# Fused chunk attention, gated mixing and feed-forward: a gate through tanh, the norm's Newton steps on GpSimd, totals of squares with bf16 ones

## The chip, the cores and the metric

One core of a Trainium2 chip. The time is the device time of one execution in microseconds; the kernel before has a median of 771.5 us over three runs (769.86 to 771.7).

## The reference, cut to what matters

```python
# attention: 4 batches, 8 heads, 768 tokens, head size 64; chunks of 32 queries, each
# sees 16 tokens to the left, its own 32, 8 to the right and 8 memory keys
a = np.exp(scores - max); out = (a / (a.sum() + 1e-9)) @ v_full
x = out as [4, 768, 512]
# gated mixing
gate_pre = sum over k of conv_w[k] * xp[:, k:k+S, :]        # 5 taps
gate = 1.0 / (1.0 + np.exp(-gate_pre))
x = gate * (x @ w_val) @ w_out
# norm and feed-forward
xn = (x - mu) / np.sqrt(var + 1e-06) * g_ln
return x + np.maximum(xn @ w_ch1, 0.0) @ w_ch2              # 512 -> 2048 -> 512
```

## The kernel before

The 3072 tokens are cut into 24 sub-blocks of 128 tokens, and these into 13 blocks: the first and the last have one sub-block, the eleven between have two. Nearly every matmul takes operands that were split into a high and a low float16 half (three products for one), with power-of-two scales that come from sums of squares.

Three streams work on each block. `attention` (from line 222) handles one sub-block in eight steps: sums of squares on ScalarE, their total over the partitions by a matmul with a tile of ones (`totals`, line 127, tile `tot`), the split of q, k and v, the scores, an Exp on ScalarE (line 286), the softmax, and the product with v. Its probabilities `p` go through a DMA transpose to `pT` before the product `pv`. `mix` (line 356) computes the five taps of the gate into `gt` (lines 366 and 370), a Sigmoid over it (line 373), the value product `val` (line 386), their product (line 388), its split into `hg` (lines 391 and 392), the output product `yps` (line 403), and then the norm of each sub-block: `y` (line 408), `bn_stats` and `bn_aggr` to `mv` (lines 411 and 412), the variance `va` (414), a first guess `rt` of 1/sqrt from the exponent bits (417 and 419), three Newton steps on it (422 to 424), all on [128, 1] tiles on VectorE, and the normalised row `xh` (427), which is split into two halves (438 on ScalarE, 439 on VectorE) and goes through two DMA transposes to `xn`. The halves have one buffer, so that those of a block's second sub-block wait for the transposes of the first. `ffn` works on chunks of hidden features: `ch1` fills one of two PSUM banks `c_ps` (line 458), ScalarE and VectorE evict it as the two halves of `h` (lines 461 and 463), and `ch2` multiplies them with the second weight into `acc` (line 478). The last chunk of a block has no later product to hide behind: its `ch2` follows the one before it at once. Of each three products of `ch2` the first two take the half of `h` that ScalarE writes, the third the one of VectorE.

The streams are laid out as generators; two strings, `PLAN` for the opening and `STEADY` for each later block, say in which order their steps are issued, mixing one block ahead of the feed-forward and attention two. A scheduler then sets the final order on each engine, and each engine runs its list in order. During the opening the weights, which arrive as float64 words, are turned into float32 (lines 148 and 149), summed (`gram`) and split (lines 198 and 199).

GpSimd has little to do: constants at the start, a maximum over the partitions (line 522), and one small copy or memset per sub-block (lines 314 and 316).

```python
for _ in range(3):
    nc.vector.scalar_tensor_tensor(out=tt, in0=rt, scalar=rt, in1=va, op0=ALU.mult, op1=ALU.mult)
    nc.vector.tensor_scalar(out=tt, in0=tt, scalar1=-0.5, scalar2=1.5, op0=ALU.mult, op1=ALU.add)
    nc.vector.tensor_tensor(out=rt, in0=rt, in1=tt, op=ALU.mult)
```

Of the kernel before, what the change touches and what calls it, by code (L numbers as in the profile page):

```python
# [18 lines left out]
P = 128  # L19
LEFT, RIGHT, CHUNK, MEM = 16, 8, 32, 8  # L20
PSCALE = 14
MID = 15
# [19 lines left out]
def passes(a, b):  # L42
    """The products that make up a @ b: of two whole operands the one, of two operands
    that were split into a high and a low half all but that of the low halves."""
    return [(a[0], b[0])] if len(a) == 1 else [(a[i], b[j]) for i, j in PASSES]
# [3 lines left out]
def chunk_attention_moe_kernel(ctx: ExitStack, tc: tile.TileContext,  # L49
# [31 lines left out]
    # ---------------------------------------------------------------- constants  # L81
    ones = const.tile([P, P], F32, name="ones")
# [10 lines left out]
    # Weights: n pieces of 1024 columns. Float32 piece i lies in slots 2i+1 and 2i+2; its  # L93
    # halves (float16) take slots 2i and 2i+1, the second one written over its source.
# [21 lines left out]
    # Powers of two from sums of squares: s with |x| s <= 2**bits for every x of the  # L116
    # sum, and 1/s, both put together from the exponent bits.
# [8 lines left out]

    def totals(cols, n):
        t = ps.tile([P, 512], F32, tag="ps", name="tot")
        nc.tensor.matmul(out=t[:, 0:n], lhsT=ones, rhs=cols, start=True, stop=True)
        return t[:, 0:n]  # L130

    # float64 to float32. The words are loaded from two bytes on, so that of each number
    # the first word holds bits 47..16 and the next 16 bits are the top: sign, 11 bits of
    # exponent, 4 of mantissa. Read as bfloat16 and written as float16, the top loses the
    # three bits of exponent that float32 lacks; the rest of the mantissa then joins it.
# [17 lines left out]
    # Room for a raw piece: most of them wait in the slots of the last weight.  # L153
# [14 lines left out]
    # Sum of squares of all pieces: the diagonal of their products with themselves.  # L168
    def gram(W, j):
# [4 lines left out]
        # the upper halves of the words, bfloat16 cut off below, are near enough for a scale  # L174
# [5 lines left out]
    def weight_scale(W, bits, name, factor=None):  # L180
# [8 lines left out]
        nc.tensor.matmul(out=W.acc[:, P:P + 1], lhsT=ones, rhs=col, start=True, stop=True)  # L189
# [11 lines left out]
    # ---------------------------------------------------------------- attention  # L201
    # A block is one or two sub-blocks of 128 tokens, whatever their batches.
# [19 lines left out]
    def attention(n, d, u):  # L222
        """Steps of one sub-block of 128 tokens (two groups of two chunks, four pairs of
        heads); x lands in place u of block d."""
# [49 lines left out]
        # A chunk sees 64 of its group's 96 keys: the first chunk the first 64, the second the last.  # L274
# [12 lines left out]
        # keys before the sequence and behind it were filled with its own: they count for nothing  # L287
# [56 lines left out]
    # ---------------------------------------------------------------- gated mixing, norm  # L344
# [11 lines left out]
    def mix(j):  # L356
# [16 lines left out]
        nc.scalar.activation(out=gt[:, :, 0:T], in_=gt[:, :, 0:T], func=AF.Sigmoid)  # L373
# [6 lines left out]
        for w in range(2):  # L380
            t = ps.tile([P, 2, 256], F32, tag="ps", name="val")
            for u in range(2):
                fc = 2 * w + u
                todo = [p for kc in range(KC) for p in passes(Wv.rows(kc, split, fc * P, P), [x[:, kc, 0:T] for x in d["x"]])]
                for x, (l, r) in enumerate(todo):
                    nc.tensor.matmul(out=t[:, u, 0:T], lhsT=l, rhs=r, start=(x == 0), stop=(x == len(todo) - 1))  # L386
            fs = slice(2 * w, 2 * w + 2)
            nc.vector.scalar_tensor_tensor(out=gt[:, fs, 0:T], in0=t[:, :, 0:T], scalar=2.0 ** -MID if split else 1.0,  # L388
                                           in1=gt[:, fs, 0:T], op0=ALU.mult, op1=ALU.mult)
            if split:  # L390
                nc.scalar.activation(out=h[0][:, fs, 0:T], in_=gt[:, fs, 0:T], func=AF.Copy)  # L391
                nc.vector.tensor_tensor(out=h[1][:, fs, 0:T], in0=gt[:, fs, 0:T], in1=h[0][:, fs, 0:T],
                                        op=ALU.subtract)
# [288 lines left out]
```

## Time and profile before

| | |
|---|---|
| timed runs | 771.5 us median (769.86 to 771.7) |
| span of the profiled execution, first to last instruction | 772.0 us; it has no separate device time |
| PE busy | 719.4 us (93%), 6412 matmuls |
| PEld (weight loads) busy | 503.0 us (65%) |
| DVE (VectorE) busy | 552.7 us (72%), 1308 instructions |
| ACT (ScalarE) busy | 456.0 us (59%), 758 instructions |
| POOL (GpSimd) busy | 9.0 us (1%), 35 instructions |
| chain that ended last | PE 73%, DVE 12%, ACT 9%, issue 4%, DMA 2% |
| granted TensorE clock, mean | 0.969 |

PE is TensorE's matmuls, L458 is line 458 of the kernel before. Busy time alone does not tell what bounds a stretch: the timeline of the stretch and the waits in it do. Ends of matmuls are modelled in the profile; the distance from one start to the next is what a matmul in a row costs.

### The profile page before, as it was taken

The page shows a single profiled execution, that of the slowest core. Times are in us where ns is not written, and L with a number is a line of the kernel's source. Part 1 is how long each engine was busy: PE and PEld are TensorE (multiplying, and loading weights), DVE is VectorE, ACT ScalarE, POOL GpSimd, SP SyncE. Part 2 cuts the span into 40 slices and gives each one's busy share as a digit, 9 for nine tenths or more (in the row PEclk, how much of TensorE's full clock was granted, in tenths as well). Part 3 has the DMA queues.
Part 4 walks back from the last instruction along what each step waited for, and adds up shares of the span by engine and source line. Part 5 has one row for each costly group of instructions (what it writes and reads, how often), then busy time and mean ns, then how long its engine had stood idle before and what let it go on. Part 6 is the DMA issues. An engine that isn't in the chain of part 4 may idle for free.

```text
span 772.0 us, 15717 instructions
## 1 busy us (share of the span) xinstructions
PE 719.4 (93%) x6412; PEld 503.0 (65%) x6412; DVE 552.7 (72%) x1308; ACT 456.0 (59%) x758; POOL 9.0 (1%) x35
## 2 busy tenths in 40 slices
PE   1567996999999999999999999999999999999997
PEld 1446853665776776766767766766766766766675
DVE  3788998898776876876876886786786787672321
ACT  5997995876773763764764664674575564531110
POOL 2000000000000000000000000000000000000000
PEclk9685997999999999999999999999999999999999
DMA  7877624214213223223223122223223111011010
GB/s 291 310 306 286 246 62 91 76 44 101 90 50 89 69 74 71 63 76 70 62 76 70 62 77 69 69 79 74 62 79 84 45 27 44 15 21 35 2 42 14
DMA packets 69735, 68.92 MB, mean 89 GB/s; under 512 B 53280, under 2 KB 53280, under 8 KB 69664
## 3 DMA queue, kind: packets, MB, share of 16 engines
q1 hardware_dynamic: 69376, 67.91, 29.6%
q8 instruction: 50, 0.82, 0.4%
q14 instruction: 21, 0.17, 0.1%
q10 hardware_dynamic: 288, 0.02, 0.0%
HBM read 49.30 MB, written 6.29 MB: 72 GB/s over the span
## 4 chain that ended last, share of the span: by engine, by line
PE 73%; DVE 12%; ACT 9%; issue 4%; DMA 2%; POOL 0%; DVEq 0%; POOLq 0%; ACTq 0%
PE c_ps L458 29%; PE acc L478 27%; PE yps L403 7%; PE val L386 4%; PE s_ps L268 3%; DVE gt L370 2%; PE pv L325 2%; DMA xn<-xh 1%; ACT top L148 1%; DVE w L149 1%; ACT w L198 1%; DMA pT<-p 1%; DVE w L199 1%; ACT sc L280 1%; ACT L286 1%
## 5 line engine op out<-in xcount | busy, mean ns | idle before, releaser
L478 PE MATMUL acc<-w,h 128*128 128x512 f16 (+1 forms) x1136 | 266.0, 385 | 0.2 <-DVE h L463 0.2
L458 PE MATMUL c_ps<-xn,w 128*128 128x256 f16 (+1 forms) x2304 | 258.8, 270 | 6.5 <-DMA xn<-xh 6.5
L458 PEld LDWEIGHTS <-w 128*128 128x128 f16 x2304 | 217.2, 99 | 44.5 <-DMA xn<-xh 7.3
L478 PEld LDWEIGHTS <-h 128*128 128x128 f16 x1104 | 106.4, 98 | 113.6 <-DVE h L463 0.7
L461 ACT ACTIVATE h<-c_ps 128x512 f16<-128x512 f32 (+1 forms) x96 | 56.7, 590 | 81.1 <-PE c_ps L458 80.0
L463 DVE SCALAR_TENSOR_TENSOR h<-c_ps,h 128x512 f16<-128x512 f32 x92 | 63.1, 685 | 52.8 <-ACT h L461 52.7
L370 DVE SCALAR_TENSOR_TENSOR gt<-xT,cw_sb,gt 128x256 f32<-128x256 f32 (+1 forms) x208 | 82.3, 455 | 0.1
L403 PE MATMUL yps<-wo,hg 128*128 128x512 f16 x276 | 63.5, 379 | 0.0
L386 PE MATMUL val<-x,wv 128*128 128x256 f16 (+1 forms) x576 | 62.4, 268 | 0.5 <-ACT x L340 0.5
L386 PEld LDWEIGHTS <-wv 128*128 128x128 f16 x576 | 54.4, 98 | 7.0 <-issue 0.7
L280 ACT ACTIVATE sc<-s_ps 64x256 f32<-64x256 f32 x96 | 36.3, 378 | 24.8 <-PE s_ps L268 23.9
L234 ACT ACTIVATE vs<-vt 128x1024 bf16<-128x1024 f32 x24 | 25.1, 1048 | 42.3 <-PE pv L325 40.7
L403 PEld LDWEIGHTS <-hg 128*128 128x128 f16 x276 | 26.9, 100 | 29.6
L268 PE MATMUL s_ps<-ks,bd 128*128 128x96 f16 x576 | 32.1, 215 | 11.6 <-ACT bd L249 8.0
L485 DVE SCALAR_TENSOR_TENSOR y<-acc,co_w,y 128x512 f32<-128x512 f32 x23 | 16.3, 747 | 36.9 <-PE acc L478 36.9
L268 PEld LDWEIGHTS <-bd 128*128 128x128 f16 x576 | 30.1, 103 | 16.3 <-issue 12.9
L438 ACT ACTIVATE xh<-xh 128x512 f16<-128x512 f32 x23 | 14.3, 623 | 43.3 <-DVE xh L427 40.1
L249 ACT ACTIVATE bd<-qt,s 64x512 f16<-64x512 f32 x48 | 34.2, 713 | 5.0 <-DVE s L122 4.3
L250 DVE SCALAR_TENSOR_TENSOR bd<-qt,s,bd 64x512 f16<-64x512 f32 x48 | 35.7, 743 | 1.1 <-ACT bd L249 0.3
L391 ACT ACTIVATE hg<-gt 128x512 f16<-128x512 f32 (+1 forms) x24 | 14.6, 611 | 31.7 <-DVE gt L388 31.6
L335 DVE TENSOR_SCALAR xT<-pv,c_pv 64x256 f32<-64x256 f32 x44 | 19.7, 489 | 19.0 <-ACT xT L333 18.7
L258 DVE SCALAR_TENSOR_TENSOR vs<-vt,s,vs 128x1024 f16<-128x1024 f32 x24 | 30.7, 1278 | 0.3 <-ACT vs L257 0.3
(119 smaller groups left out, 813.5 us busy)
## 6 DMA issues: line engine op xcount, KB each, us to landing
vt<-in_v_dram SPq DMA_DIRECT2D x24, 512.0 KB, 4.1
kt<-in_k_dram SPq DMA_DIRECT2D x24, 384.0 KB, 3.7
w<-in_w_ch_dram SPq DMA_DIRECT2D x8, 1023.8 KB, 8.0
qt<-in_q_dram SPq DMA_DIRECT2D x24, 256.0 KB, 2.7
out_dram<-y SPq DMA_DIRECT2D x24, 256.0 KB, 2.0
w<-in_w_ch_dram SPq DMA_DIRECT2D x5, 1023.5 KB, 7.1
raw<-in_w_ch_dram SPq DMA_DIRECT2D x3, 1023.5 KB, 11.2
w<-in_w_val_dram SPq DMA_DIRECT2D x2, 1023.5 KB, 9.0
```

The lines of the kernel that those rows point to most:

```text
L249: nc.scalar.activation(out=hi, in_=src, func=AF.Copy, scale=s[pp, 0:1])
L250: nc.vector.scalar_tensor_tensor(out=lo, in0=src, scalar=s[pp, 0:1], in1=hi, op0=ALU.mult, op1=ALU.subtract)
L258: nc.vector.scalar_tensor_tensor(out=v2[1], in0=vt, scalar=s[:, 2:3], in1=v2[0], op0=ALU.mult, op1=ALU.subtract)
L268: nc.tensor.matmul(out=t[:, hp, :], lhsT=bd[r0][:, hp, g].rearrange("p c e q -> p (c e q)"), rhs=k2[r1][:, hp, g, :], start=(x == 0), stop ...
L280: nc.scalar.activation(out=by_group[pp, :, g, :], in_=s_ps[g][pp, :, ch * CHUNK:ch * CHUNK + NSEEN], func=AF.Copy)
L370: nc.vector.scalar_tensor_tensor(out=o, in0=xT[:, hp, 0:n, kk:kk + SUB], scalar=cw_sb[:, kk, hp:hp + 1], in1=o, op0=ALU.mult, op1=ALU.add)
L386: nc.tensor.matmul(out=t[:, u, 0:T], lhsT=l, rhs=r, start=(x == 0), stop=(x == len(todo) - 1))
L403: nc.tensor.matmul(out=t, lhsT=l, rhs=r, start=(x == 0), stop=(x == len(todo) - 1))
L458: nc.tensor.matmul(out=t[:, u * T:(u + 1) * T], lhsT=l, rhs=r, start=(x == 0), stop=(x == len(todo) - 1))
L461: nc.scalar.activation(out=h[0], in_=t, func=AF.Relu)
L463: nc.vector.scalar_tensor_tensor(out=h[1], in0=t, scalar=0.0, in1=h[0], op0=ALU.max, op1=ALU.subtract)
L478: nc.tensor.matmul(out=a, lhsT=l, rhs=r, start=(m == 0 and x == 0), stop=(m == NM - 1 and x == len(todo) - 1))
```

## The change

Three edits; no comment or empty line that was taken out counts.

1. The gate. The Sigmoid becomes Tanh with a scale of 0.5, the product with `val` becomes (1 + tanh) times `val`, and the half goes into a later factor (`cy_w`, or 0.5 for the first block); the factor 2^-MID moves into the two splitting instructions, with MID at 16 for 15.
2. The norm. The three Newton steps move from VectorE (three instructions a step) to GpSimd (four a step, twelve per sub-block); the first guess takes one VectorE instruction for two.
3. The totals. The tile of ones is bfloat16, and the matmul reads the upper halves of the float32 words of the sums as bfloat16; the same for the totals of the weights.

```diff
-    ones = const.tile([P, P], F32, name="ones")
+    ones = const.tile([P, P], BF16, name="ones")
+    def upper(cols):
+        return cols.bitcast(BF16).rearrange("p (n w) -> p n w", w=2)[:, :, 1]
...
-        nc.tensor.matmul(out=t[:, 0:n], lhsT=ones, rhs=cols, start=True, stop=True)
+        nc.tensor.matmul(out=t[:, 0:n], lhsT=ones, rhs=upper(cols), start=True, stop=True)
...
-        nc.scalar.activation(out=gt[:, :, 0:T], in_=gt[:, :, 0:T], func=AF.Sigmoid)
+        nc.scalar.activation(out=gt[:, :, 0:T], in_=gt[:, :, 0:T], func=AF.Tanh, scale=0.5)
...
-            nc.vector.scalar_tensor_tensor(out=gt[:, fs, 0:T], in0=t[:, :, 0:T], scalar=2.0 ** -MID if split else 1.0,
-                                           in1=gt[:, fs, 0:T], op0=ALU.mult, op1=ALU.mult)
+            nc.vector.scalar_tensor_tensor(out=gt[:, fs, 0:T], in0=gt[:, fs, 0:T], scalar=1.0, in1=t[:, :, 0:T],
+                                           op0=ALU.add, op1=ALU.mult)
             if split:
-                nc.scalar.activation(out=h[0][:, fs, 0:T], in_=gt[:, fs, 0:T], func=AF.Copy)
-                nc.vector.tensor_tensor(out=h[1][:, fs, 0:T], in0=gt[:, fs, 0:T], in1=h[0][:, fs, 0:T],
-                                        op=ALU.subtract)
+                nc.scalar.activation(out=h[0][:, fs, 0:T], in_=gt[:, fs, 0:T], func=AF.Copy, scale=2.0 ** -MID)
+                nc.vector.scalar_tensor_tensor(out=h[1][:, fs, 0:T], in0=gt[:, fs, 0:T], scalar=2.0 ** -MID,
+                                               in1=h[0][:, fs, 0:T], op0=ALU.mult, op1=ALU.subtract)
...
-            nc.vector.tensor_scalar(out=tt.bitcast(I32), in0=va.bitcast(I32), scalar1=1, scalar2=None,
-                                    op0=ALU.logical_shift_right)
-            nc.vector.tensor_scalar(out=rt.bitcast(I32), in0=tt.bitcast(I32), scalar1=-1.0,
+            nc.vector.tensor_scalar(out=rt.bitcast(I32), in0=va.bitcast(I32), scalar1=-0.5,
                                     scalar2=float(0x5f3759df), op0=ALU.mult, op1=ALU.add)
             for _ in range(3):
-                nc.vector.scalar_tensor_tensor(out=tt, in0=rt, scalar=rt, in1=va, op0=ALU.mult, op1=ALU.mult)
-                nc.vector.tensor_scalar(out=tt, in0=tt, scalar1=-0.5, scalar2=1.5, op0=ALU.mult, op1=ALU.add)
-                nc.vector.tensor_tensor(out=rt, in0=rt, in1=tt, op=ALU.mult)
+                nc.gpsimd.tensor_tensor(out=tt, in0=rt, in1=rt, op=ALU.mult)
+                nc.gpsimd.tensor_tensor(out=tt, in0=tt, in1=va, op=ALU.mult)
+                nc.gpsimd.tensor_scalar(out=tt, in0=tt, scalar1=-0.5, scalar2=1.5, op0=ALU.mult, op1=ALU.add)
+                nc.gpsimd.tensor_tensor(out=rt, in0=rt, in1=tt, op=ALU.mult)
```

The order of the instructions, first on VectorE, at the second norm of a block in the later part (`mv` and `va` are the mean and variance, `rt` and `tt` the Newton step's tiles, `h` the evicted chunk, the last three rows the normalised row and its low half and the block's last chunk). Before, from the first guess of `rt` on:

```order
L419 TENSOR_SCALAR rt<-tt 128x1
L422 SCALAR_TENSOR_TENSOR tt<-rt,va 128x1
L423 TENSOR_SCALAR tt<-tt 128x1
L424 TENSOR_TENSOR rt<-rt,tt 128x1
L422 SCALAR_TENSOR_TENSOR tt<-rt,va 128x1
L423 TENSOR_SCALAR tt<-tt 128x1
L463 SCALAR_TENSOR_TENSOR h<-c_ps,h 128x512
L424 TENSOR_TENSOR rt<-rt,tt 128x1
L422 SCALAR_TENSOR_TENSOR tt<-rt,va 128x1
L423 TENSOR_SCALAR tt<-tt 128x1
L424 TENSOR_TENSOR rt<-rt,tt 128x1
L427 TENSOR_SCALAR xh<-y,mv,rt 128x512
```

Now, in the changed kernel, whose lines stand five further down from here on (L423 is the first guess, L432 the row `xh`, L444 its low half, L468 the eviction of `h`):

```order
L417 BN_AGGR mv<-bs 128x2
L422 TENSOR_SCALAR va<-mv 128x1
L423 TENSOR_SCALAR rt<-va 128x1
L468 SCALAR_TENSOR_TENSOR h<-c_ps,h 128x512
L432 TENSOR_SCALAR xh<-y,mv,rt 128x512
L444 TENSOR_TENSOR xh_3690<-xh,xh_3689 128x512
L468 SCALAR_TENSOR_TENSOR h<-c_ps,h 128x512
```

Between the guess and `xh` only one eviction is left on VectorE, and the block's last eviction stands behind `xh` and its low half.

At the first norm of the same block, now:

```order
L423 TENSOR_SCALAR rt<-va 128x1
L468 SCALAR_TENSOR_TENSOR h<-c_ps,h 128x512
L432 TENSOR_SCALAR xh<-y,mv,rt 128x512
L288 TENSOR_REDUCE mx<-sc 128x8
L444 TENSOR_TENSOR xh_3624<-xh,xh_3623 128x512
L289 TENSOR_TENSOR sc<-sc,mx 128x512
```

The two softmax instructions (L288 and L289, lines 284 and 285 before) stood ahead of `xh` in the kernel before and stand behind it now.

On GpSimd, at the first norm of the program:

```order
L318 MEMSET xT 128x4x4
L320 COPY xT<-xT 128x4x4
L426 ISA
L426 TENSOR_TENSOR tt<-rt 128x1
L427 TENSOR_TENSOR tt<-tt,va 128x1
L428 TENSOR_SCALAR tt<-tt 128x1
L429 TENSOR_TENSOR rt<-rt,tt 128x1
```

The row ISA, which loads code, is new and stands once; the four rows behind it are one of the three Newton steps, and each of the twelve instructions waits for the one before it.

On ScalarE the 26 table loads of the kernel before (`ACT_TABLE_LOAD`, one at the start, then one ahead of each Sigmoid and one ahead of the next Exp) become one, at the start. On PE the order is the same from the third block's feed-forward on; ahead of that some products have changed places.

## Rows read from the trace of the kernel before

**Rows 1.** Busy time per stretch; columns: us, PE, PEld, DVE, ACT, POOL busy, PEclk, DMA share, GB/s

```profile
0.00:193.00 193.00, 145.69 (x1327) 106.08 (x1327) 159.23 (x351) 150.82 (x228) 5.87 (x18) 0.88 0.53 181
193.00:680.00 487.00, 485.74 (x4375) 337.53 (x4376) 364.98 (x882) 290.37 (x508) 3.17 (x17) 1.00 0.25 65
```

**Rows 2.** What PE waited for from 193 us on: total, times, longest

```profile
PE pv L325 <- DMA pT<-p: 0.8, 1, 0.8
```

**Rows 3.** Timeline of PE in one later block: start us, us, instruction, count

```profile
280.49 0.28 PE L129 MATMUL tot<-ss,ones 128*128 128x3 f32 x2
280.63 2.75 PE L403 MATMUL yps<-wo,hg 128*128 128x512 f16 x12
...
299.86 5.34 PE L478 MATMUL acc<-w,h 128*128 128x512 f16 x24
305.14 0.87 PE L325 MATMUL pv<-pT,vs 64*128 64x64 f16 x48
```

**Rows 4.** Timeline of DVE in the same block: start us, us, instruction, [idle before]

```profile
270.78 0.69 DVE L296 TENSOR_REDUCE sum<-sc 128x8 f32<-128x512 f32 x1 [1.34 <-ACT sc L286]
...
271.95 0.69 DVE L299 TENSOR_TENSOR sc<-sc,rs 128x512 f32<-128x512 f32 x1
273.33 0.69 DVE L302 TENSOR_TENSOR p<-sc,p 128x512 f16<-128x512 f32 x1 [0.69 <-ACT p L301]
...
287.21 0.15 DVE L417 TENSOR_SCALAR tt<-va 128x1 int32<-128x1 int32 x1
...
290.37 0.69 DVE L285 TENSOR_TENSOR sc<-sc,mx 128x512 f32<-128x512 f32 x1
...
291.91 0.69 DVE L296 TENSOR_REDUCE sum<-sc 128x8 f32<-128x512 f32 x1 [0.39 <-ACT sc L286]
...
294.93 0.69 DVE L302 TENSOR_TENSOR p<-sc,p 128x512 f16<-128x512 f32 x1
295.55 0.17 DVE L412 BATCH_NORM_AGGREGATE mv<-bs 128x2 f32<-128x6 f32 x1
...
295.94 0.15 DVE L417 TENSOR_SCALAR tt<-va 128x1 int32<-128x1 int32 x1
...
298.70 0.55 DVE L427 TENSOR_SCALAR xh<-y,mv,rt 128x512 f32<-128x512 f32 x1
299.99 0.69 DVE L439 TENSOR_TENSOR xh<-xh,xh 128x512 f16<-128x512 f32 x1 [0.74 <-ACT xh L438]
300.69 0.69 DVE L463 SCALAR_TENSOR_TENSOR h<-c_ps,h 128x512 f16<-128x512 f32 x1
```

**Rows 5.** Timelines of ACT, DVE and PE around the second block's norm, same columns

```profile
110.59 1.28 ACT L286 ACT_TABLE_LOAD   x1
...
112.18 0.15 DVE L414 TENSOR_SCALAR va<-mv 128x1 f32<-128x1 f32 x1
...
118.00 0.54 DVE L427 TENSOR_SCALAR xh<-y,mv,rt 128x512 f32<-128x512 f32 x1
...
120.72 0.55 DVE L427 TENSOR_SCALAR xh<-y,mv,rt 128x512 f32<-128x512 f32 x1
...
128.90 4.84 PE L458 MATMUL c_ps<-xn,w 128*128 128x256 f16 x23 [1.92 <-DMA xn<-xh]
```

**Rows 6.** Groups by line: the table loads ahead of the Sigmoids; busy us, mean ns

```profile
L373 ACT ACT_TABLE_LOAD x13 | 16.7, 1283 | 0.2
```

**Rows 7.** Timelines of POOL and DVE: start us, us, instruction, [idle before]

```profile
22.61 0.45 POOL L522 PARTITION_ALL_REDUCE g_max<-g_one  x1 [6.30 <-DVE wv_col L186]
...
38.91 0.20 POOL L316 COPY xT<-xT 128x16 f32<-128x16 f32 x1 [15.80 <-ACT xT L333]
...
99.04 0.11 POOL L314 MEMSET xT<- 128x16 f32 x1 [8.27 <-DVE gt L370]
...
307.57 0.90 DVE L335 TENSOR_SCALAR xT<-pv,c_pv 64x256 f32<-64x256 f32 x2 [1.56 <-ACT xT L333]
308.52 0.20 POOL L316 COPY xT<-xT 128x16 f32<-128x16 f32 x1 [27.57 <-DVE xT L335]
```

More of the change, by code (lines that the diff above doesn't have):

```diff
@@ L21 @@
 PSCALE = 14
-MID = 15
+MID = 16
 NTOP = 2
@@ L188, in weight_scale @@
             nc.vector.tensor_tensor(out=col, in0=col, in1=factor, op=ALU.mult)
-        nc.tensor.matmul(out=W.acc[:, P:P + 1], lhsT=ones, rhs=col, start=True, stop=True)
+        nc.tensor.matmul(out=W.acc[:, P:P + 1], lhsT=ones, rhs=upper(col), start=True, stop=True)
         pow2(W.acc[:, P:P + 1], 1, bits, s, inv)
@@ L403, in mix @@
                 nc.tensor.matmul(out=t, lhsT=l, rhs=r, start=(x == 0), stop=(x == len(todo) - 1))
-            c_y = 1.0
+            c_y = 0.5
             if split:
@@ L413, in mix @@
             va = sm_p.tile([P, 1], F32, tag="va", name="va")
-            nc.vector.tensor_scalar(out=va, in0=mv[:, 1:2], scalar1=1e-6, scalar2=None, op0=ALU.add)
             rt = sm_p.tile([P, 1], F32, tag="rt", name="rt")
             tt = sm_p.tile([P, 1], F32, tag="tt", name="tt")
-            nc.vector.tensor_scalar(out=tt.bitcast(I32), in0=va.bitcast(I32), scalar1=1, scalar2=None,
-                                    op0=ALU.logical_shift_right)
-            nc.vector.tensor_scalar(out=rt.bitcast(I32), in0=tt.bitcast(I32), scalar1=-1.0,
+            nc.vector.tensor_scalar(out=va, in0=mv[:, 1:2], scalar1=1e-6, scalar2=None, op0=ALU.add)
+            nc.vector.tensor_scalar(out=rt.bitcast(I32), in0=va.bitcast(I32), scalar1=-0.5,
                                     scalar2=float(0x5f3759df), op0=ALU.mult, op1=ALU.add)
             for _ in range(3):
-                nc.vector.scalar_tensor_tensor(out=tt, in0=rt, scalar=rt, in1=va, op0=ALU.mult, op1=ALU.mult)
-                nc.vector.tensor_scalar(out=tt, in0=tt, scalar1=-0.5, scalar2=1.5, op0=ALU.mult, op1=ALU.add)
-                nc.vector.tensor_tensor(out=rt, in0=rt, in1=tt, op=ALU.mult)
+                nc.gpsimd.tensor_tensor(out=tt, in0=rt, in1=rt, op=ALU.mult)
+                nc.gpsimd.tensor_tensor(out=tt, in0=tt, in1=va, op=ALU.mult)
+                nc.gpsimd.tensor_scalar(out=tt, in0=tt, scalar1=-0.5, scalar2=1.5, op0=ALU.mult, op1=ALU.add)
+                nc.gpsimd.tensor_tensor(out=rt, in0=rt, in1=tt, op=ALU.mult)
             yield
@@ L551, in mixing_weights @@
             so, io = weight_scale(Wo, 15, "wo")
-            nc.vector.tensor_scalar(out=cy_w, in0=iv, scalar1=io, scalar2=2.0 ** MID, op0=ALU.mult, op1=ALU.mult)
+            nc.vector.tensor_scalar(out=cy_w, in0=iv, scalar1=io, scalar2=2.0 ** (MID - 1), op0=ALU.mult, op1=ALU.mult)
             yield
```

## The prediction

> **What bounds the kernel now.** I read the busy times of two stretches first. From 193 us to 680 us PE is busy for 485.74 of 487.00 us at a granted clock of 1.00, while DVE has 364.98 and ACT 290.37 [rows 1]. Nothing is gained there by relieving DVE or ACT: only what shortens PE's own row of products counts, or a new wait of PE. Before 193 us PE has 145.69 of 193 us at a mean clock of 0.88, DVE 159.23 and ACT 150.82: here PE waits, and work taken off the other two can come through. The second view is what PE waited for from 193 us on: one wait above half a microsecond, 0.8 us on the transposed probabilities [rows 2]. Then I read one later block on PE and DVE [rows 3, 4], because the change puts a chain of twelve GpSimd instructions into DVE's order, and the block's last eviction stands behind it. Last come the norm of the second block in the opening [rows 5], the table loads [rows 6], and the few things that GpSimd does today [rows 7]. The sum is made against the span of 772.0 us, which is 0.5 us above the median of the timed runs; a difference under 0.3%, 2.3 us, cannot be told from none.
>
> **Totals.** A total starts at 280.49 and the next product at 280.63 [rows 3]: 0.14 us for two passes over 128x3 columns. One pass is left, which now loads its weights: between half of it and all of it is saved, 0.07 to 0.14; I take 0.10, nearer to half. Seventeen of the 24 totals lie behind 193 us: 17 x 0.10 = **-1.7 us** (1.2 to 2.4).
>
> **Table loads.** Thirteen stand ahead of the Sigmoids, 1.283 us each [rows 6], and 13 others ahead of an Exp or at the start; one load remains in all. Behind 193 us ACT has some 197 us free, and the loads that go there were hidden by PE. Only the 0.8 us wait on `pT` [rows 2] has two of them upstream, in the Sigmoid and the Exp of the same block: 2 x 1.283 is more than 0.8, so I take **-0.8 us** (0 to 0.8).
>
> The Trainium skill, "ScalarE: Activation LUTs", section "What ACT_TABLE_LOAD costs", puts a switch of tables at about 1283 ns and a drain of about 1380 ns besides. The rows have the 1283; no row here has a drain as an entry of its own. By the page the switch that leaves the opening's path would give 1.4 us more, and the sum would be 766.1.
>
> **The opening.** The second block's feed-forward takes its last `xn` at 128.90, after PE has been idle 1.92 us [rows 5]. Ahead of it stand, in one chain, an Exp's table load (1.28 at 110.59), `va` at 112.18, and the two `xh` at 118.00 and 120.72. Between `va` and the first `xh` lie 5.8 us of DVE work, among them 20 small instructions of both norms' Newton steps, which I put at 0.08 us each net of their overlap, 1.6 us (bound: 0.15 each, 3.0, as the first guess takes [rows 4]). With the load and these gone the first `xh` starts some 3 us earlier, near 115.0. The halves of the second `xh` wait for the transposes of the first, so that the second follows by the same amount. The first block's norm, at 55 to 67 us, holds 1.5 us more of the same kind upstream. Together **-4.5 us**. The ends: -1.0, if other DVE work fills the gaps, and -6.5, if the small instructions cost their full duration and all idle time goes. It is less by whatever the GpSimd chain takes above the 2.95 us that I put in below.
>
> **The chain on GpSimd.** DVE loses ten short instructions a sub-block; from 193 us on that is work off the path, worth nothing. In their place `xh` waits for twelve GpSimd instructions, each behind its predecessor, and DVE goes in order: behind `xh` are queued its low half and the eviction of the block's last `h`, for which PE waits. I call C the time from the end of the first guess to the start of `xh`. In the block shown [rows 4] the first guess would end at 287.36 (start 287.21 plus 0.15). From there to the block's last eviction the new order has, by the spacings of today's rows: first C; `xh` to its low half 1.29 (298.70 to 299.99); on to the softmax's subtraction 0.62 (294.93 to 295.55, as between two full instructions); subtraction to sum, with the Exp between, 1.54 (290.37 to 291.91); sum to the scaled row 1.17 (270.78 to 271.95); to `p` 1.38 (271.95 to 273.33); to `mv` 0.62; `mv` to the end of the second guess 0.54 (295.55 to 296.09). These are 7.16. Then C again, and from `xh` to the end of `h` 1.29 + 0.70 + 0.69 = 2.68. So the last `h` is ready at 287.36 + 7.16 + 2.68 + 2C = 297.2 + 2C. PE needs it at the third product of the second half of its last 24, the 15th: 299.86 + 14 x 0.22 (5.28 / 24) = 302.9 [rows 3], and 0.1 sooner for the total. **Up to C = 2.80 us nothing is lost; above it the block loses twice the rest.** There are ten such blocks: nine of two sub-blocks behind 193 us, and the one just before.
>
> What is C? Today GpSimd has no arithmetic on such tiles. The nearest rows are a copy of 128x16, 0.20 us, which starts 0.05 after the DVE instruction it waits for ends (308.47 to 308.52), and a memset of 128x16, 0.11 us [rows 7]. Reading one operand thus costs at most 0.09. A step with one operand is then about 0.23 with its hand-over (C = 2.81 if all twelve were so cheap), one with two operands up to 0.32. Nine of the twelve have two: 9 x 0.32 + 3 x 0.23 + 0.05 = 3.62. I take a mean step of 0.24, by the copy, which is the nearest row and larger than 128x1: C = 12 x 0.24 + 0.05 = 2.93, say 2.95, a stall of 2 x 0.15 = 0.30 a block, **+3.0 us** for ten (0 to 16.4).
>
> The new ISA row, a code load, has no time in this trace. GpSimd's first wait for other code could be the 6.30 us of idle time ahead of its reduction [rows 7], though that row names DVE as its releaser. The load stands behind the copy of 38.91, and the first Newton step is not due before 55 us: even 6.30 us ends at 45.4. It costs nothing; without that cover it would be 6.30 once.
>
> The (1 + tanh) product is the same instruction with other operations and the two splits gain a factor: nothing.
>
> **Sum:** 772.0 - 1.7 - 0.8 - 4.5 + 3.0 = 768.0, or **767.5 us** as a timed run. This case's own range is 763 to 769: with C at 2.81 the stall goes almost to zero, and 764.6 is left; the opening's outer end takes it to 763.
>
> **Rival 1: the chain becomes the bound, slower.** Every step with two operands takes 0.32 us: C = 3.62, the stall is 2 x 0.82 = 1.64 a block, 16.4 for ten; the opening gives 3.8 only. 772.0 - 1.7 - 0.8 - 3.8 + 16.4 = 782.1, **781.6** timed. It decides early: gains and stall balance at C = 3.14, a mean step of 0.258 us. For it: a step needs its predecessor's result written and signalled, and no row shows two dependent GpSimd instructions in a row. Against it: the copy took 0.196 with 16 columns, these have one.
>
> For this rival also speaks the Trainium skill, "GPSIMD Engine Reference", section 2.1 Instruction dispatch: the two reads of a two-operand instruction share one SBUF read port there, and elementwise work belongs on DVE. No row of this trace has such an instruction, so it stays untested until the next.
>
> **Rival 2: the opening gives nothing, no change.** DVE has 159 of 193 us there, full of conversions and softmax work, and the streams are ordered by a fixed plan: what goes from the norm may only be waited out elsewhere, or each of the twelve instructions is held up behind one of DVE's. Then 772.0 - 1.7 - 0.8 + 3.0 = 772.5, **772.0** timed. Against it: PE's 1.92 us wait in front of 128.90 is on the very chain that is shortened.
>
> **Rival 3: the loads stay.** If Tanh and Exp were not in one table, 26 loads would stand and 1.28 of the opening would not come. The order of the changed program holds one load; I leave it out.
>
> **Chances.** My case 0.45, rival 1 0.35, rival 2 0.20. So faster by over 0.3% 0.45, within 0.3% 0.20, slower 0.35. The range takes in my case from its lower end and rival 1 with a little above its value: 763 to 783; about one in ten lies above, as C has no upper bound in the rows, and less below.
>
> **What would show it.** Right: GpSimd's Newton instructions 0.2 to 0.25 us from start to start; DVE idle ahead of `xh`, released by GpSimd, with 2.9 to 3.0 us from guess to `xh` less the eviction between; PE waiting about 0.3 us for DVE's `h` in the last products of each block; the wait on `pT` gone; one table load; a total's product and the next 0.03 to 0.07 apart; the second block's first features at about 124 in place of 128.9. Wrong: waits of PE on `h` of 0.8 us and more per block (rival 1), or the second block still at 128 (rival 2); and if PE waits nowhere and C is 3.5, the slack of 2.80 was worked out wrongly.

## The result, and the profile after

The changed kernel takes 782.3 us (three runs, 781.43 to 785.31) against 771.5: a ratio of 1.0146 (95% interval 1.0109 to 1.0183), slower by 10.8 us. The forecast was 767.5 with a range from 763 to 783: the time lies inside the range, but on the other side of no change.

| | before | after |
|---|---|---|
| span of the profiled execution | 772.0 | 779.6 |
| PE busy | 719.4 | 717.8 |
| DVE busy | 552.7 | 517.1 |
| ACT busy | 456.0 | 421.9 |
| POOL busy | 9.0 | 68.0 |
| table loads on ACT | 26 | 1 |
| one later block, from its value product to the next (the commonest value) | 56.41 | 57.15 |

A timed run lies 1.9 us above its own span, as the runs below show (770.36 against 768.4 for the kernel of E1). The trace of before, 772.0, was therefore one of its slower executions, some 773.9 as a timed run (an estimate); the two spans differ by 7.6 us, the medians by 10.8.

The same two stretches as in [rows 1], columns as there:

```profile
0.00:193.00 193.00, 142.65 (x1265) 102.03 (x1266) 151.55 (x300) 142.06 (x221) 21.31 (x78) 0.94 0.53 181
193.00:680.00 487.00, 479.45 (x4323) 329.27 (x4322) 335.86 (x706) 262.42 (x480) 39.79 (x209) 1.00 0.26 65
```

DVE and ACT have lost 29 and 28 us of work behind 193 us, and PE does 52 products fewer in the same 487 us, 17 of them the second passes of the totals. What PE waited for from 193 us to 690 us (total, times, longest), which answers to [rows 2]:

```profile
PE acc L483 <- ACT h L466: 4.7, 8, 0.7
PE acc L483 <- DVE h L468: 1.9, 8, 0.2
PE c_ps L463 <- DMA xn<-xh: 0.9, 3, 0.4
```

The wait on `pT` is gone, and eight blocks have a new one, for both halves of the last `h`. The end of one of them on PE, as [rows 3] (start, duration, instruction, count, idle before):

```profile
301.45 2.75 PE L483 MATMUL acc<-w,h 128*128 128x512 f16 x12
304.76 0.61 PE L483 MATMUL acc<-w,h 128*128 128x512 f16 x2 [0.55 <-ACT h L466]
305.60 2.33 PE L483 MATMUL acc<-w,h 128*128 128x512 f16 x10 [0.24 <-DVE h L468]
307.86 0.87 PE L329 MATMUL pv<-pT,vs 64*128 64x64 f16 x48
```

From the first product of `acc` to `pv` are 6.41 us; before, the same 24 took 5.28 (299.86 to 305.14, [rows 3]). The block loses 1.13 us, more than the 0.79 that the waits list, because ends of products are modelled. The same block on GpSimd and on DVE ([rows 4] and [rows 7] of before), first the second of its two chains of twelve, then DVE around it, then ACT:

```profile
299.73 0.19 POOL L426 TENSOR_TENSOR tt<-rt 128x1 f32<-128x1 f32 x1 [7.21 <-DVE rt L423]
300.00 0.19 POOL L427 TENSOR_TENSOR tt<-tt,va 128x1 f32<-128x1 f32 x1
300.27 0.19 POOL L428 TENSOR_SCALAR tt<-tt 128x1 f32<-128x1 f32 x1
300.55 0.19 POOL L429 TENSOR_TENSOR rt<-rt,tt 128x1 f32<-128x1 f32 x1
...
302.73 0.19 POOL L429 TENSOR_TENSOR rt<-rt,tt 128x1 f32<-128x1 f32 x1
```

```profile
299.49 0.15 DVE L423 TENSOR_SCALAR rt<-va 128x1 int32<-128x1 int32 x1
299.56 0.68 DVE L468 SCALAR_TENSOR_TENSOR h<-c_ps,h 128x512 f16<-128x512 f32 x1
302.95 0.55 DVE L432 TENSOR_SCALAR xh<-y,mv,rt 128x512 f32<-128x512 f32 x1 [2.71 <-POOL rt L429]
304.25 0.69 DVE L444 TENSOR_TENSOR xh<-xh,xh 128x512 f16<-128x512 f32 x1 [0.74 <-ACT xh L443]
304.86 0.69 DVE L468 SCALAR_TENSOR_TENSOR h<-c_ps,h 128x512 f16<-128x512 f32 x1
```

```profile
303.58 0.63 ACT L443 ACTIVATE xh<-xh 128x512 f16<-128x512 f32 x1 [4.64 <-issue]
304.12 0.58 ACT L466 ACTIVATE h<-c_ps 128x512 f16<-128x512 f32 x1
```

An instruction lasts 0.19 us, and the next starts 0.27 us after it did (299.73, 300.00, 300.27, 300.55): 0.08 us lie between. From the end of the guess (299.64) to `xh` (302.95) are 3.31 us, the C of the prediction. DVE is idle for 2.71 of them, ACT for 4.64 from 298.94 on, and on both the block's last eviction stands behind the two halves of `xh`: ACT's at 304.12, DVE's at 304.86. PE's two waits end with these two.

In the opening the second block's last `xn` lets PE start at 122.23 in place of 128.90 [rows 5], 6.7 us earlier. Some 3.4 us of this lead are there from the start: the first block's value product begins at 35.90, before at 39.30. At the start GpSimd builds the tile `eye` and fills the tile `top`, for which ScalarE waits with the first weights. Before, then in the changed kernel:

```profile
13.34 0.28 POOL L514 TENSOR_SCALAR_AFFINE_SELECT eye<-eye 128x128 f32<-128x128 f32 x1 [11.51 <-issue]
14.56 1.34 ACT L148 ACTIVATE top<-w 128x1024 f16<-128x1024 bf16 x1 [2.75 <-POOL top L517]
```

```profile
2.12 0.29 POOL L519 TENSOR_SCALAR_AFFINE_SELECT eye<-eye 128x128 f32<-128x128 f32 x1 [0.29 <-POOL top L522]
10.92 1.33 ACT L152 ACTIVATE top<-w 128x1024 f16<-128x1024 bf16 x1
```

Before, GpSimd is idle for 11.51 us ahead of the first row, released by nothing that the profile shows; in the changed kernel it is not. All runs below divide in the same way. In the eight kernels with Newton steps on GpSimd in any block this row starts at 2.12 and the first value product at 34.6 to 36.7; in the eight others the row starts at 13.0 to 14.0 and the product at 39.2 to 40.3. What fills the 11.5 us no row shows, so why they go stays open. At the end of the third block the lead is gone:

```profile
122.23 2.69 PE L463 MATMUL c_ps<-xn,w 128*128 128x256 f16 x23 [0.70 <-DMA xn<-xh]
...
183.28 3.19 PE L483 MATMUL acc<-w,h 128*128 128x512 f16 x14
189.75 3.89 PE L483 MATMUL acc<-w,h 128*128 128x512 f16 x10 [3.28 <-DVE h L468]
```

```profile
188.55 0.55 DVE L432 TENSOR_SCALAR xh<-y,mv,rt 128x512 f32<-128x512 f32 x1 [3.31 <-POOL rt L429]
189.01 0.68 DVE L468 SCALAR_TENSOR_TENSOR h<-c_ps,h 128x512 f16<-128x512 f32 x1
```

```profile
190.00:194.00 4.00, 4.00 (x40) 1.56 (x40) 1.57 (x3) 0.00 (x0) 0.00 (x0) 0.63 0.33 66
194.00:200.00 6.00, 6.00 (x83) 5.25 (x75) 3.94 (x12) 4.89 (x9) 0.20 (x1) 1.00 0.25 90
```

PE waits 3.28 us for the last `h`, whose eviction at 189.01 stands behind an `xh` that waited 3.31 us for GpSimd. Then ten products take 3.89 us, where the last ten of the 24 in a later block take 2.33 (at 305.60 above): the granted clock is 0.63 in 190 to 194 and 1.00 behind it, so another 1.6 us go at the lower of the two levels (1.2 for 2.4 GHz).

### The profile page after: what moved, and what is told of

Same layout as the page of the kernel before. It is cut to its first block, busy times and chain, and to the rows that moved or that the text cites. A ratio compares the mean times of both kernels' runs of the same rounds, so it can differ in the third digit from the quotient of the medians.

```text
span 779.6 us, 15675 instructions
## 1 busy us (share of the span) xinstructions
PE 717.8 (92%) x6384; PEld 495.1 (64%) x6384; DVE 517.1 (66%) x1068; ACT 421.9 (54%) x733; POOL 68.0 (9%) x323
## 4 chain that ended last, share of the span: by engine, by line
PE 49%; DVE 20%; ACT 13%; issue 10%; POOL 5%; DMA 3%; SPq 0%; ACTq 0%; DVEq 0%
PE c_ps L463 22%; PE acc L483 17%; PE val L391 6%; DVE gt L374 2%; DMA xn<-xh 2%; ACT vs L238 2%; PE s_ps L272 2%; DVE xh L444 1%; DVE vs L262 1%; ACT xh L443 1%; ACT w L202 1%; PE yps L408 1%; DVE bd L254 1%; POOL tt L426 1%; POOL tt L427 1%
## 5 line engine op out<-in xcount | busy, mean ns | idle before, releaser
L483 PE MATMUL acc<-w,h 128*128 128x512 f16 (+1 forms) x1136 | 272.0, 388 | 11.9 <-DVE h L468 7.2
L468 DVE SCALAR_TENSOR_TENSOR h<-c_ps,h 128x512 f16<-128x512 f32 x92 | 63.1, 686 | 50.2 <-ACT h L466 50.2
L432 DVE TENSOR_SCALAR xh<-y,mv,rt 128x512 f32<-128x512 f32 x24 | 13.1, 546 | 62.5 <-POOL rt L429 62.5
L426 POOL TENSOR_TENSOR tt<-rt 128x1 f32<-128x1 f32 x72 | 15.4, 214 | 314.3 <-DVE rt L423 288.8
```

Source lines behind the costliest of these rows:

```text
L468: nc.vector.scalar_tensor_tensor(out=h[1], in0=t, scalar=0.0, in1=h[0], op0=ALU.max, op1=ALU.subtract)
L483: nc.tensor.matmul(out=a, lhsT=l, rhs=r, start=(m == 0 and x == 0), stop=(m == NM - 1 and x == len(todo) - 1))
```

## Experiments

"Period" is the distance from one block's first value product to the next one's, the mean of the eight distances from the fourth block to the twelfth; "fourth block" is where the first value product behind 193 us starts in the profiled run. Ratios are to the kernel before, run beside it on the same chip. Profiles, and so the last two columns, are of one execution each.

| run | what it is | median us | ratio (95%) | fourth block | period |
|---|---|---|---|---|---|
| before | | 771.5 | | 215.16 | 56.45 |
| after | all three edits | 782.3 | 1.0146 (1.0109 to 1.0183) | 216.30 | 57.38 |
| E1 | edits 1 and 3, Newton on DVE | 770.71 | 0.9991 (0.9975 to 1.0006) | 216.03 | 56.02 |
| E2 | edit 2 alone | 790.8 | 1.0242 (1.0223 to 1.026) | 223.65 | 57.42 |
| E3 | edit 1 alone | 773.37 | 1.0019 (1.0006 to 1.0033) | 215.09 | 56.24 |
| E4 | edit 3 alone | 770.67 | 0.9979 (0.997 to 0.9988) | 213.84 | 56.25 |
| E5 | after, 16 instructions on GpSimd | 815.87 | 1.0557 (1.0532 to 1.0582) | 223.46 | 60.86 |
| E6 | after, 6 instructions on GpSimd | 780.83 | 1.0108 (1.0085 to 1.0131) | 213.68 | 57.55 |
| E7 | after, GpSimd from the fourth block on | 779.66 | 1.0092 (1.0067 to 1.0117) | 212.86 | 57.41 |
| E8 | after, 6 instructions on DVE | 773.93 | 1.0009 (0.9987 to 1.0031) | 218.24 | 56.02 |
| E9 | after, last eviction ahead of `xh` | 779.4 | 1.0098 (1.0074 to 1.0121) | 220.89 | 56.77 |
| E10 | E9 with E6's 6 instructions | 774.94 | 1.0035 (1.0023 to 1.0048) | 214.65 | 56.69 |
| E11 | E4 with 6 instructions on DVE | 771.29 | 0.9988 (0.9977 to 0.9999) | 213.42 | 56.37 |
| E12 | after, GpSimd in the first three blocks only | 771.85 | 1.0004 (0.9986 to 1.0022) | 216.00 | 56.02 |
| E13 | E1, Sigmoid in the first three blocks | 770.19 | 0.9966 (0.9951 to 0.998) | 217.05 | 56.02 |
| E14 | E1, Sigmoid from the fourth block on | 774.42 | 1.0028 (1.0012 to 1.0045) | 220.05 | 56.26 |

The theory after the result: what is lost is the GpSimd chain, since the block's last eviction is queued behind it. Rivals: a fixed price of handing a value to GpSimd and back; one of the other two edits; a GpSimd at work that slows DVE.

### E1 to E4: the edits apart

E1 is the changed kernel with this, E2 the reverse in the kernel before, E3 and E4 take edit 1 and edit 3 of the diff above alone.

```diff
-                nc.gpsimd.tensor_tensor(out=tt, in0=rt, in1=rt, op=ALU.mult)
-                nc.gpsimd.tensor_tensor(out=tt, in0=tt, in1=va, op=ALU.mult)
-                nc.gpsimd.tensor_scalar(out=tt, in0=tt, scalar1=-0.5, scalar2=1.5, op0=ALU.mult, op1=ALU.add)
-                nc.gpsimd.tensor_tensor(out=rt, in0=rt, in1=tt, op=ALU.mult)
+                nc.vector.scalar_tensor_tensor(out=tt, in0=rt, scalar=rt, in1=va, op0=ALU.mult, op1=ALU.mult)
+                nc.vector.tensor_scalar(out=tt, in0=tt, scalar1=-0.5, scalar2=1.5, op0=ALU.mult, op1=ALU.add)
+                nc.vector.tensor_tensor(out=rt, in0=rt, in1=tt, op=ALU.mult)
```

> The changed kernel with the Newton steps back on VectorE (three instructions a step), the one-instruction guess, the tanh gate and the bf16 totals kept. Theory A (all that was lost is the GpSimd chain: 0.8 us a block from 216 us on, and the wait of 3.3 us with the clock drop behind it at the end of the third block): both waits vanish, the block period falls from 57.15 to about 56.3 us, time 766 to 769. Rival B (the tanh gate or the totals themselves put work or a worse order in the way): time at 771 or above, period still above 56.4.

> The kernel before with edit 2 alone: Newton steps on GpSimd, guess in one instruction, Sigmoid and f32 totals kept. Theory A: the block period rises from 56.41 to about 57.3 (stall 0.85, totals as before), time 781 to 785, at or a little above the changed kernel. Rival B: the loss needs the other edits, time under 777.

> The kernel before with edit 1 alone (tanh gate, its half folded away; Newton on VectorE with the two-instruction guess, f32 totals). Theory A: 0.8 us of the wait on pT and up to 3 us of the opening, time 768 to 771. Rival B: 772 or more.

> The kernel before with edit 3 alone (bf16 ones, totals in one pass). Theory A: start to next start of a total falls from 0.14 to 0.03 us, 17 x 0.11 = 1.9 us less behind 193 us, time 769 to 770. Rival B: no gain or a loss, 771 to 773.

E1's period is 56.02, a little below the 56.3 expected, and PE's only waits behind 193 us are two on `xn`:

```profile
PE c_ps L462 <- DMA xn<-xh: 1.3, 2, 0.9
```

```profile
300.05 5.34 PE L482 MATMUL acc<-w,h 128*128 128x512 f16 x24
305.33 0.87 PE L329 MATMUL pv<-pT,vs 64*128 64x64 f16 x48
...
308.77 0.17 PE L133 MATMUL tot<-ss,ones 128*128 128x3 bf16 x1
308.79 1.47 PE L462 MATMUL c_ps<-xn,w 128*128 128x256 f16 x12
```

The 24 products take 5.28 us again, and a total 0.02 to 0.03 where it took 0.14 [rows 3]. From the fourth block to the twelfth E1 takes 448.1 us and the changed kernel 459.0: these 10.9 us are nearly all of the 11.2 between the two spans. But E1's time is 770.7, not 766 to 769: from the fourth block to the end of the trace it is 4.4 us shorter than the kernel before, 3.4 of it in eight periods of 0.43, and the time is only 1.3 us less by the medians (by the ratio not told from none). So its opening lost most of what the later part gained. E3 says the same of the tanh gate alone: 0.21 us less per block, and yet 1.4 us more in all; the expectation of 768 to 771 missed. E4 gains 1.6 us by the ratio, near the 1.9 expected; its time lies above 769 to 770 because the kernel before took 772.0 beside it. E2 is 18.8 us slower, 8 more than all three edits together and beyond the 781 to 785 expected: its period (57.42) is that of the changed kernel, and its fourth block is 8.5 us late (223.65). The chain costs the opening more without the other two edits; how they meet there was not taken further. Edit 2 is the loss, edit 3 a gain, edit 1 a gain in the later blocks and a loss in the opening.

### E5, E6: the chain's length

E5 is `range(4)` for `range(3)`. E6 does the three steps in six instructions:

```diff
-                                    scalar1=1e-6, scalar2=None, op0=ALU.add)
+                                    scalar1=1e-6, scalar2=-0.5, op0=ALU.add, op1=ALU.mult)
...
-                                    scalar2=float(0x5f3759df), op0=ALU.mult, op1=ALU.add)
+                                    scalar2=float(0x5f3759df - 2 ** 22 - 2 ** 30), op0=ALU.mult, op1=ALU.add)
             for _ in range(3):
+                nc.gpsimd.tensor_scalar(out=tt, in0=rt, scalar1=rt, scalar2=va, op0=ALU.mult, op1=ALU.mult)
+                nc.gpsimd.tensor_scalar(out=rt, in0=tt, scalar1=1.5, scalar2=rt, op0=ALU.add, op1=ALU.mult)
```

> The changed kernel with a fourth Newton step on GpSimd, sixteen instructions for twelve (the result is the same number). Theory A (PE loses twice the chain's length above 2.80 us in each block): the chain from guess to xh grows by 4 x 0.272 = 1.09 us to 4.4, the block's stall from 1.13 to 3.3, the period from 57.15 to 59.3; behind 193 us that is 9 x 2.2 = 20 us, with the opening's third block 2 to 3 more: 803 to 808. Rival (a fixed price of handing a value to GpSimd and back): 782 to 787.

> The changed kernel with the same three Newton steps on GpSimd in six instructions for twelve (two operands of a tensor_scalar come from [128, 1] columns, the factor -0.5 lies in va and the guess's constant). Theory A: the chain is 6 x 0.27 + 0.05 = 1.7 us, under 2.80, so no stall: period 56.0, no wait of PE for h behind 193 us, time 768 to 772. Rival (fixed hand-over): period at 56.6 or more, 776 or more. If an instruction with columns as scalars takes twice as long, the chain is at 3.3 and the time stays at 782.

E5 on PE, the end of one block, and the clock in it:

```profile
310.95 2.75 PE L483 MATMUL acc<-w,h 128*128 128x512 f16 x12
316.61 0.60 PE L483 MATMUL acc<-w,h 128*128 128x512 f16 x2 [2.90 <-ACT h L466]
317.45 3.83 PE L483 MATMUL acc<-w,h 128*128 128x512 f16 x10 [0.24 <-DVE h L468]
321.21 0.88 PE L329 MATMUL pv<-pT,vs 64*128 64x64 f16 x48
```

```profile
316.00:322.00 6.00, 5.16 (x60) 2.16 (x60) 2.63 (x4) 0.55 (x2) 0.00 (x0) 0.72 0.22 44
```

From 310.95 to 321.21 are 10.26 us, 4.98 over the 5.28. Of these 1.50 are the ten products at 317.45, which take 3.83 for 2.33 at a granted clock that falls to 0.72 in this stretch; 3.48 are the wait. Against 1.13 in the changed kernel that is 2.35 for four instructions in each of two chains, 8 x 0.27 = 2.2: the slope is as expected, the rival of a fixed price falls. The time (815.9) is above the expected 808 for two reasons. The clock was not in the sum: behind six of the eight such waits the ten products take 3.64 to 4.02 us, some 1.5 us more each. And the fourth block stands 7.2 us later than in the changed kernel, for which 2 to 3 had been put in. The length of the wait alone does not tell where the clock falls: behind the first and the last of the eight waits, 2.90 us each, the ten take 2.33, and the first period is 59.5 and the last 60.3 where those between are 61.0 to 61.3. The changed kernel's waits of 0.8 us have no such sequel (its clock is 1.00 from 193 us to 680 us).

E6 missed, in two ways. Its chain is longer than six plain instructions, and the order on DVE is another one, set by the scheduler from its own durations. GpSimd, DVE and PE:

```profile
297.54 0.34 POOL L426 TENSOR_SCALAR tt<-rt,va 128x1 f32<-128x1 f32 x1 [8.15 <-DVE rt L423]
297.98 0.27 POOL L427 TENSOR_SCALAR rt<-tt,rt 128x1 f32<-128x1 f32 x1
298.34 0.34 POOL L426 TENSOR_SCALAR tt<-rt,va 128x1 f32<-128x1 f32 x1
```

```profile
297.28 0.15 DVE L423 TENSOR_SCALAR rt<-va 128x1 int32<-128x1 int32 x1
299.89 0.55 DVE L430 TENSOR_SCALAR xh<-y,mv,rt 128x512 f32<-128x512 f32 x1 [2.45 <-POOL rt L427]
300.35 0.68 DVE L466 SCALAR_TENSOR_TENSOR h<-c_ps,h 128x512 f16<-128x512 f32 x1
...
301.74 0.69 DVE L466 SCALAR_TENSOR_TENSOR h<-c_ps,h 128x512 f16<-128x512 f32 x1
```

```profile
301.09 4.92 PE L481 MATMUL acc<-w,h 128*128 128x512 f16 x22 [1.31 <-DVE h L466]
```

An instruction that takes both factors from columns lasts 0.34, and the next starts 0.44 us after it did; with one factor from a column it is 0.27 and 0.36. So six take 2.46 us from the guess's end (297.43) to `xh` (299.89). That is under the 2.80 of the prediction, and still the block loses 1.5 us (57.50 for 56.02 in most blocks): now the eviction of the last chunk but one, at 300.35, stands behind `xh` too, PE needs that one earlier and waits 1.31 us for it. The threshold of 2.80 belongs to one order of DVE. That the shorter chain is what moved the scheduler was not tested by itself.

### E7, E12: where the loss lies

The Newton steps go to GpSimd for `j > 2` (E7) or for `j < 3` (E12) alone, to VectorE in the other blocks.

> The changed kernel with GpSimd's Newton steps only from the fourth block of mixing on, the first three on VectorE. Theory A (the loss lies in the later blocks): the opening is that of the kernel with the steps on VectorE (first value product behind 193 us at 216), then periods of 57.15: 770.7 + 9 x 1.13 = 780 to 782. Rival (a good part is lost in the opening): 772 to 777.

> The changed kernel with GpSimd's Newton steps in the first three blocks of mixing alone, VectorE's from the fourth on. Theory A: the period is 56.0 behind 216 us, and what is left is the price of the chain in the opening: 2 to 3 us above the kernel with all of them on VectorE, 772 to 775. Rival (the opening pays nothing): 769.5 to 771.5.

E7 less E1 is 1.0 +- 0.3%, 5.6 to 10 us, and the changed kernel less E1 1.55 +- 0.4%. Both hide a gain: E7, E12 and the changed kernel have GpSimd's early start, E1 has not. E7's Newton steps are on VectorE for the whole opening, as E1's are, yet its first value product starts at 35.71 (E1 39.55) and its fourth block at 212.86, not at the 216 that was expected. From the fourth block to the twelfth it then loses 11.1 us against E1, as the changed kernel does (10.9). That is where the loss lies.

The chain has a price in the opening as well: the fourth block of the changed kernel starts at 216.30, 3.4 us behind E7's, and the times agree (the changed kernel less E7 is 0.5 +- 0.4%, 0.7 to 7.6 us). E12 less E1 is 0.13 +- 0.23%, at the lower edge of what was expected and not told from nothing, but the opening does not come for nothing there. E12's first value product starts at 35.06, 4.5 us ahead of E1's. At the third block the lead is 2.9 us (154.21 and 157.06), PE then waits 3.27 us for the last `h`, and at the fourth both are at 216.0: what the early start gives, the chain takes.

### E8, E11: six instructions on VectorE

The two lines of E6 with `nc.vector`, in the changed kernel (E8) and beside edit 3 alone (E11).

> The same six instructions on VectorE, tanh gate and bf16 totals kept. Theory A: period 56.0 as with nine instructions there; only the opening can gain from three to five fewer short instructions a sub-block: 768 to 770.7. Rival (the opening is bound by other work): 770 to 772, equal to the nine instructions.

> The kernel before with the bf16 totals and the six-instruction Newton steps on VectorE, the Sigmoid kept: a candidate for the best. Period 56.2 as with the totals alone, time 768 to 770.7 if fewer short instructions help the opening, 770.5 to 772 if not.

E8's period is E1's to the hundredth: in the later blocks DVE's short instructions are free. Its median, 773.9, is above both ranges, but its ratio is not told from E1's (0.2 +- 0.3%): it spreads from 768.09 to 776.56, and the runs at 774 and more have a granted clock of 0.964 to 0.967 where those at 769 have 0.991. E11 gains no more than E4 does.

### E9, E10: another place for the last eviction

`xh` of the second norm is made to wait for the block's last `h`, and its step is issued behind that chunk, so that the eviction goes ahead of it on DVE; E10 has E6's chain besides.

```diff
+            last = blk[j - 1].get(("h", 7)) if j and u == 1 else None
+            if last:
+                nc.vector.tensor_copy(out=xh[:, 0:1], in_=last[1][:, 0:1])
             nc.vector.tensor_scalar(out=xh, in0=y[:, u, :], scalar1=mv[:, 0:1], scalar2=rt,
...
-... x2 f1 a1 f3 a1 f1 a2"
+... x1 f1 a1 f3 x1 a1 f1 a2"
```

> The changed kernel with all twelve GpSimd instructions, but the block's last eviction placed ahead of the second norm's xh on VectorE: a copy of one column of that h into xh, which xh then writes over, makes xh wait for it. Theory A (what costs 1.13 us a block is that the last eviction stands behind an instruction that waits for GpSimd): the wait of PE for h goes, the period falls from 57.15 to between 56.0 and 56.4 (xh and its transposes now come late for the next block by up to 0.4), time 773 to 776. Rival (GpSimd at work slows VectorE or the evictions themselves, wherever they stand): period stays at 57, time 780 or more.

> The same placing with the six-instruction chain on GpSimd (2.46 us as measured, for 3.32). Theory A: period 56.0, no wait of PE in the later blocks, 769 to 774, level with the Newton steps on VectorE. Rival: 777 or more.

E9's waits, and one block's end in it:

```profile
PE c_ps L466 <- DMA xn<-xh: 4.6, 8, 0.9
PE acc L486 <- DVE h L471: 3.3, 1, 3.3
```

```profile
248.90 5.34 PE L486 MATMUL acc<-w,h 128*128 128x512 f16 x24
254.17 0.87 PE L329 MATMUL pv<-pT,vs 64*128 64x64 f16 x48
...
255.75 2.69 PE L466 MATMUL c_ps<-xn,w 128*128 128x256 f16 x23 [0.49 <-DMA xn<-xh]
```

With all twelve GpSimd instructions the 24 products take 5.27 us: the wait for `h` is gone, so it came from the place in the queue and not from a GpSimd that slows DVE. What was not expected in size is the next wait: `xh` and its transposes are now late for the following block by 0.5 us on the first chunk, and the period is 56.7, not 56.4 or less. The one wait for `h` that stays in the list, 3.3 us, is the third block's, which this edit did not reach. The time is 779.4 instead of 773 to 776, although the eight later blocks take 4.9 us less than in the changed kernel: E9's fourth block starts at 220.89, 4.6 us behind the changed kernel's, and from the twelfth block to the thirteenth it takes 1.5 us more. Why the opening is later stays open; the changed kernel has the third block's wait too. E10, with a chain 0.86 us shorter, has the same 56.7, for `xh` waits for the eviction in both; no wait for `h` is left behind 193 us, but the period is not the 56.0 expected, and its 774.9 is just above the 769 to 774 and above E1's 770.7.

### E13, E14: the tanh gate in the opening

The gate is Sigmoid with the kernel before's scales for the first three blocks (E13) or from the fourth on (E14); otherwise as E1.

> Newton steps on VectorE, bf16 totals; the tanh gate from the fourth block of mixing on, the Sigmoid in the first three. Theory A (the tanh gate's order in the opening takes back some 3 us): the opening of the kernel before or of the totals alone, then periods of 56.0: 767 to 769, the fastest of all. Rival (the opening is bound by other work, the gate has no part): 770 to 771.5, level with the tanh gate everywhere.

> The reverse: tanh gate in the first three blocks, Sigmoid from the fourth on; Newton steps on VectorE, bf16 totals. Theory A: the tanh gate's opening and periods of 56.2: 772 to 774. Rival: 770 to 771.5.

E14 less E13 is 0.62 +- 0.22%, 4.8 us. From the fourth block to the end of the trace E14 takes 2.9 us more, and the rest, 1.9 +- 1.7 us, is what the tanh gate costs in the opening; in the traces its fourth block is 3.0 us later. So part of the opening's gain is taken back by the gate itself. The traces show where: at the third block PE waits 1.87 and 1.95 us for `pT` in E14 (at 151.58 and 173.37), 0.74 and 0.35 in E13 (at 148.54 and 170.12), 2.7 us less. What makes `pT` late with the gate stays open; the scheduler sets another order there, but one move that I suspected, three weight splits on DVE between the softmax's subtraction and `p` where the kernel before has two, stands in E13 as in E14. E13 has the lowest ratio of the study, 0.9966 (0.9951 to 0.998) of before, though its 770.19 is not the 767 to 769 expected: bf16 totals, Newton on VectorE, tanh from the fourth block on. E4's interval overlaps with its own.

## Why the prediction was wrong, step by step

**What bounds it.** Right: behind 193 us only PE's own row and new waits counted. DVE's and ACT's 57 us less there (rows above) are worth no more than the 0.2 us a block of edit 1 (E3), and DVE's short instructions nothing (E8 beside E1).

**Totals.** Right: 0.11 us each by the trace against 0.10, and E4's 1.6 us (0.21%) against 1.7.

**Table loads in the later blocks.** Too small. The list of PE's waits named one, of 0.8 us. E3's period is 0.21 us shorter, some 2 us in all: in the kernel before one `pv` of each block was slow as well (1.04 us at 276.91 where the other takes 0.87 at 305.14; in E3 both take 0.87), in short gaps that the list of waits leaves out.

**The opening.** The first step that failed. "Together -4.5 us" was read off the second block, and there it came: PE's first full chunk starts at 124.61 in E1, 4.3 us earlier than 128.90. The prediction let this lead run through to the end. By the fourth block E1 stands at 216.03, before at 215.16. In E1 the lead goes at the third block, in waits for the transposed probabilities. PE's waits for them between 130 and 193 us, before and then in E1:

```profile
PE pv L325 <- DMA pT<-p: 1.1, 2, 0.6
PE pv L329 <- DMA pT<-p: 4.1, 3, 1.9
```

They are 3.0 us longer, and as the last two of them end (169.84 and 171.15) the granted clock is 0.61 from 170 to 174 us, which takes up to 1.6 more (4.00 x 0.39, an estimate); before, it is 1.00 there. PE came early, and DVE, which writes `p`, did not: the `p` of the third block's second wait starts at 167.47 in E1, at 166.81 before. In the changed kernel it is the GpSimd chain itself: PE reaches the third block's last 24 products at 183.28, 2.7 us earlier than before (185.98), but DVE's eviction comes at 189.01, before at 188.66. A lead on one engine is worth what the next meeting with the other engines leaves of it, and this one was not looked up.

**The code load.** Put at nothing, and PE has no wait from the new row. But the prediction took 6.30 us for GpSimd's first wait that could be one for code, where the same trace has the 11.51 us shown above ahead of it; with the change these went, and 3.4 us of them came through to the first value product. Whether they are code is not shown, but this gain was in no term. In the changed kernel the chain took it back, so that it stands at 216.30 at the fourth block: the opening gave nothing.

**The chain.** The second step that failed. The mechanism was right and its price wrong. In "I take a mean step of 0.24, by the copy", the instruction was right (0.19, the copy 0.20), and the hand-over wrong: 0.05 had been read where GpSimd follows DVE, and from one GpSimd instruction to the next it is 0.08. The step is 0.27, C is 3.31, and the formula then gives 2 x (3.31 - 2.80) = 1.02 us a block; the trace has 1.13 in the commonest case. The waits are in eight blocks behind 193 us and in the third, not in ten. The eight lose 10.9 us against E1, where 3.0 were put in for all: five lose 1.1 to 1.3 each and the last three 1.5 to 1.8, PE waiting 0.2 to 0.4 us for `xn` in them as well.

**The rivals.** Rival 1 named the mechanism, the place and the point of balance (C = 3.14, a step of 0.258; measured 0.27, behind it), and its 781.6 is 0.7 us from the time, but by two errors that cancel: a stall of 1.64 a block (1.13) and an opening that gives 3.8 (nothing): its nearness is luck. Between a step of 0.24 and one of 0.26 the forecast changed its sign; with bounds of 0.23 and 0.30 (C of 2.81 and 3.62) from rows that far off, the chances of faster and slower should have been closer to each other, and slower ahead. Rival 2 was right about the opening by itself. With C at 3.31, the opening at nothing and its own ten blocks, the prediction's sum is 772.0 - 1.7 - 2 + 10.2 = 778.5 as a span, against 779.6; eight blocks in place of ten and a loss above the formula's in each nearly cancel.

The Trainium skill, "GPSIMD Engine Reference", section 2.1 Instruction dispatch, has the two reads of a two-operand instruction share one SBUF read port. At one column this does not show here: the one-operand instruction (L428) is no shorter than the others. The median is 0.19 us for all four, and a few longer ones, up to 1.19, lie in the norms of the first blocks (groups by line: busy, mean ns, idle before):

```profile
L426 POOL TENSOR_TENSOR tt<-rt 128x1 f32<-128x1 f32 x72 | 15.4, 214 | 314.3 <-DVE rt L423 288.8 <-DVE e L120 21.7
L428 POOL TENSOR_SCALAR tt<-tt 128x1 f32<-128x1 f32 x72 | 14.3, 199 | 6.3
L429 POOL TENSOR_TENSOR rt<-rt,tt 128x1 f32<-128x1 f32 x72 | 14.1, 196 | 6.0
```

The Trainium skill, "ScalarE: Activation LUTs", section "What ACT_TABLE_LOAD costs", adds a drain of about 1380 ns to each switch. No row shows one as an entry of its own, and E3, with one load for 26, is not faster in all, so the runs give it no support here, where most loads were off PE's path.

## What to carry to other kernels

An instruction moved to an idle engine is paid for in latency by whatever stands behind its consumer in the in-order queue: count the chain from end to start with its hand-overs, find the first instruction behind the consumer that the bounding engine needs, and compare. A lead gained early is worth only what is left of it where the engines next meet, so follow it to the end of the opening before it enters a sum. Where a scheduler sets the order from its own durations, a cheaper chain can come back with a worse order (E6), so a threshold holds for one order only. And compare the starts of two programs first: a gain there, as GpSimd's early start, can hide a loss of the same size (E12).

## What the runs showed of the hardware that was not expected

On GpSimd a [128, 1] instruction takes 0.19 us and the dependent one starts 0.27 us after it; one with both factors from columns lasts 0.34 and takes 0.44. GpSimd's 11.1 to 12.2 us of idle time ahead of its first selection are there in the eight kernels without Newton steps on it and in none of the eight with them; why is open. Behind PE's wait of 3.28 us (changed kernel) and six of eight waits of 2.90 to 3.08 us (E5), ten products took 3.64 to 4.02 us for 2.33, at a granted clock of 0.63 and 0.72 in the stretches shown: a second price of about half the wait. Behind E1's wait of 1.95 us at 169.84 the clock fell too (0.61 from 170 to 174 us). Two of E5's waits of 2.90 us, and the waits of 0.8 us, had no such sequel.
